# Strided attention and two expert layers on one core: half of a value load moved to ScalarE's queue, and the first weight chunk asked for one step earlier

## The chip, the cores and the metric

The kernel runs on one core of a Trainium2 chip. The metric is the time of one execution on the device in microseconds (us); the runs of the kernel before have their median at 618.33 us.

## The reference

All inputs are float32: q, k and v of 2 batches, 8 heads, 576 positions and 64 elements a head.

```python
scores = (q @ k.T) / sqrt(64)                 # per batch and head
mask   = (rel >= 0) & (rel < 32)              # heads 0-3, rel = i - j ("local")
mask   = (rel >= 0) & (j % 32 == i % 32)      # heads 4-7 ("strided")
attn   = softmax(where(mask, scores, -1e9)); x = attn @ v
x      = x laid out as 1152 tokens x 512
h      = ((x @ w1) * (x @ w2)) @ w3           # w1, w2: 512 x 1024, w3: 1024 x 1024
x      = h @ w_out                            # 1024 x 512
p      = domain_probs / (sum + 1e-9)          # 4 experts
out    = sum over e of p[:, e] * (relu(x @ W1[e]) @ W2[e])
```

## The kernel before

The program is one unrolled stream of instructions on each engine, in the order in which the Python code records them (a manual schedule): nothing reorders it, so what stands earlier in the source on one engine runs earlier there. The engines are TensorE (PE), VectorE (DVE), ScalarE (ACT) and GpSimd (POOL); SyncE (SP) issues nearly all loads and stores, as queue 1. ScalarE issues a few, as queue 10. Queue 8 and queue 14 carry instructions.

Attention of the first batch (`first`, six chunks; chunks 0 to 2 local heads, 3 to 5 strided heads) stands at the start and fills the first 24 us. Every chunk goes through `scores` (PE), `maxima` and `subtract` (DVE), `exps` or `slots_exps` (ACT), `sums` (DVE), `normalise` (POOL in this batch, L450), `transposes` (PE), `evac` (ACT, L460), `pv` (PE, L475 for local and L484 for strided heads) and `put` (ACT, L513). Then the product of x with w1 and w2 begins with `whole_product` (L616), which uses the first weight chunk `zero` in full float32; the other weight chunks are split into a high and a low float32r half on ACT and DVE, and the products of the second batch's attention are mixed in. After that come the combined matrix of w3 and w_out, and the experts, where PE is busy throughout.

The loads around the change, in SP's order: keys and queries of batch 0 (L322), the local values (`load_v_loc`, L330, 7 loads), the strided values (`load_v_str`, L352, two halves of 64 partitions, 320 KB each), their rest (`load_v_rest`, L357, two loads of 18 KB), then the first weight chunk (`zero.whole_load`, L160, two halves of 512 KB), the second chunk (L140), keys and queries of batch 1 (L322), and more chunks. Two things hold a load back. A load that must not start too early is tied to POOL: `hold` sets one column of its buffer (L128), and the load waits for that memset, which stands in POOL's stream behind whatever was recorded before it. And the loads take eight completion semaphores in turn (DMAHW0 to DMAHW7): the next load on a semaphore waits until the one before on it has landed.

The first weight chunk is used from `whole_steps` (DVE, L171 and on) and `whole_low` (ACT, L165).

Of the kernel before, what the change touches and what calls it, by code (L numbers as in the profile page):

```python
# [8 lines left out]
F32 = mybir.dt.float32  # L9
# [9 lines left out]
P = 128  # L19
# [25 lines left out]
def kernel(  # L45
# [13 lines left out]
    nc = tc.nc  # L59
# [10 lines left out]
    big = [tc.tile_pool(name=f"big{b}", bufs=4, side=side).__enter__() for b, side in enumerate(("right", "left"))]  # L70
# [241 lines left out]
    qk, vals = {}, {}  # L312
# [12 lines left out]
    def load_v_loc(b, c):  # L325

        tv = wp.tile([P, 2, 3, P], F32, tag="w", name="tv_loc")

        def load(dst, rows, t0, n):
            nc.sync.dma_start(out=dst, in_=v_loc[b, :, rows, t0:t0 + n].rearrange("k p t d -> p k t d"))  # L330

        lower, upper, middle = slice(0, 64), slice(64, P), slice(W, 3 * W)
        if c == 0:
            load(tv[lower, :, 0:1], lower, 0, 1)
            load(tv[upper, :, 0:1], middle, 0, 1)
            load(tv[:, :, 1:], slice(0, P), 1, 2)
        elif c == 1:
            load(tv, slice(0, P), 3, 3)
        else:
            load(tv[lower, :, 0:1], lower, 0, 1)  # L340
            load(tv[lower, :, 1:], middle, 1, 2)
            load(tv[upper], middle, 3, 3)
        vals[b, 0, c] = tv

    def load_v_str(b):

        tv = big[0].tile([P, 12, P], F32, tag="big", name="tv_str")
        row = 5 * P
        for k in range(2):
            at = v_str[b, k, 0, 0]  # L350
            rows = bass.AP(tensor=at.tensor, offset=at.offset, ap=[[row, 64], [T3 * row, 2], [1, row]])
            nc.sync.dma_start(out=tv[64 * k:64 * k + 64, :10].rearrange("p (h t) d -> p h (t d)", h=2), in_=rows)  # L352
        vals[b, 1] = tv

    def load_v_rest(b):
        for k in range(2):
            nc.sync.dma_start(out=vals[b, 1][64 * k:64 * k + NB, 10:], in_=v_str[b, k, 2 * T3:2 * T3 + NB, :2])  # L357
# [494 lines left out]
    with tc.manual_schedule():  # L852
# [5 lines left out]
        for i in range(4):  # L858
# [6 lines left out]
        load_v_loc(0, 0)  # L865
        load_v_loc(0, 1)
        load_v_loc(0, 2)
        load_v_str(0)
        load_v_rest(0)
        zero = c_w12[0]  # L870
        rest_loads = {5: [lambda: load_qk(1, 1)], 6: [lambda c=c: load_v_loc(1, c) for c in range(3)],
                      8: [lambda: load_v_str(1), lambda: load_v_rest(1)]}
        chunks = [[Chunk4(3 * g + c, b, g, c) for g in range(2) for c in range(3)] for b in range(B)]
        units = [(b, ft, i) for b in range(B) for ft in range(8) for i in range(2)]
# [52 lines left out]
        def exp_of(i):  # L927
            first[i].maxima()
            first[i].subtract()
            first[i].exps()  # L930

        def scale_of(i):
            first[i].sums()
            first[i].normalise()
# [14 lines left out]
        first[2].scores()  # L949
        first[1].maxima()  # L950
        first[1].slots_exps()
        scale_of(0)
        keep_warm(1, 2)
        first[3].scores()
# [7 lines left out]
        first[5].scores()  # L962
        first[0].pv()
        exp_of(3)
        scale_of(2)
        zero.whole_load()
        loaded = 1
        evac(1)
        first[2].transposes()
# [91 lines left out]
        for it in range(8):  # L1061
# [9 lines left out]
            if i is not None:  # L1071
# [7 lines left out]
        halves = [Tokens(0, 5, lambda name, i, n: ops.tile([P, 2, 320], F32R, tag="op", name=f"b_{name}{i}")),  # L1079
                  Tokens(5, 4, lambda name, i, n: keep(name, i, n))]  # L1080
        keeps = iter(range(9))

        def keep(name, i, n):

            k = next(keeps, None)
            if k is not None:
                return kept[:, k]
            return ops.tile([P, 2, 320], F32R, tag="op", name=f"b_{name}{i}")[:, :, :n]
# [121 lines left out]
```

## Time and profile before

| | us |
|---|---|
| median of 3 runs | 618.33 (617.79 to 619.99) |
| profiled execution, its own time | 618.26 |
| span of its trace | 616.1 |
| PE busy | 609.8 (99%) |
| DVE busy | 443.1 (72%) |
| ACT busy | 280.6 (46%) |
| POOL busy | 9.9 (2%) |

The span counts from the first to the last instruction of the core; 2.2 us of the time lie around it. Busy time is the union of an engine's instructions, weight loads of PE apart. The chain that ended last is followed backwards from the last instruction, at each step to what released it; a piece called issue is time in which the engine waited for nothing that the profile shows. The granted clock of PE is 1.00, its full level, in every stretch read here.

### The profile page before, as it was taken

The page shows a single profiled execution, that of the slowest core. Times are in us where ns is not written, and L with a number is a line of the kernel's source. Part 1 is how long each engine was busy: PE and PEld are TensorE (multiplying, and loading weights), DVE is VectorE, ACT ScalarE, POOL GpSimd, SP SyncE. Part 2 cuts the span into 40 slices and gives each one's busy share as a digit, 9 for nine tenths or more (in the row PEclk, how much of TensorE's full clock was granted, in tenths as well). Part 3 has the DMA queues.
Part 4 walks back from the last instruction along what each step waited for, and adds up shares of the span by engine and source line. Part 5 has one row for each costly group of instructions (what it writes and reads, how often), then busy time and mean ns, then how long its engine had stood idle before and what let it go on. Part 6 is the DMA issues. An engine that isn't in the chain of part 4 may idle for free.

```text
span 616.1 us, 11131 instructions
## 1 busy us (share of the span) xinstructions
PE 609.8 (99%) x4488; PEld 555.9 (90%) x4488; DVE 443.1 (72%) x811; ACT 280.6 (46%) x568; POOL 9.9 (2%) x33
## 2 busy tenths in 40 slices
PE   8999999999999999999999999999999999999997
PEld 5799999998889999998899988999889898989997
DVE  4899987998863237777877987887766665755843
ACT  3879966665733134333433333434343333333320
POOL 4100000000000000000000000000000000000000
PEclk9999999999999999999999999999999999999999
DMA  9896330334522202333545334435585557464411
GB/s 272 321 325 185 139 138 2 111 132 172 202 68 102 86 19 69 137 138 136 199 153 194 128 149 172 167 142 212 178 318 202 213 192 248 162 234 176 156 51 68
DMA packets 28510, 99.63 MB, mean 162 GB/s; under 512 B 2660, under 2 KB 6316, under 8 KB 26028
## 3 DMA queue, kind: packets, MB, share of 16 engines
q1 hardware_dynamic: 27916, 98.34, 44.5%
q8 instruction: 35, 0.57, 0.4%
q10 hardware_dynamic: 544, 0.59, 0.3%
q14 instruction: 15, 0.12, 0.1%
HBM read 79.78 MB, written 19.14 MB: 161 GB/s over the span
## 4 chain that ended last, share of the span: by engine, by line
PE 90%; DVE 4%; ACT 3%; DMA 2%; issue 1%; DVEq 0%; ACTq 0%; SPq 0%
PE g_acc L305 11%; PE g_acc L306 11%; PE g_acc L307 11%; PE m_a L307 4%; PE m_a L306 4%; PE m_a L305 4%; PE ab_acc L305 3%; PE ab_acc L307 3%; PE ab_acc L306 3%; PE m_b L306 3%; PE m_c L305 3%; PE m_c L306 3%; PE m_b L305 3%; PE x_acc L305 3%; PE m_c L307 3%; PE m_b L307 3%
## 5 line engine op out<-in xcount | busy, mean ns | idle before, releaser
L761 ACT ACTIVATE h_hi<-u 128x320 fp32r<-128x320 f32 (+1 forms) x128 | 56.9, 445 | 188.9 <-DVE u L767 188.9
L305 PE MATMUL g_acc<-w_hi,h_hi 128*128 128x512 f32 (+1 forms) x296 | 114.3, 386 | 0.0
L306 PE MATMUL g_acc<-w_lo,h_hi 128*128 128x512 f32 (+1 forms) x296 | 114.2, 386 | 0.0
L307 PE MATMUL g_acc<-w_hi,h_lo 128*128 128x512 f32 (+1 forms) x296 | 113.7, 384 | 0.0
L700 DVE TENSOR_TENSOR w_lo<-raw,w_hi 128x768 fp32r<-128x768 f32 x64 | 69.3, 1084 | 12.3 <-ACT w_hi L698 12.3
L767 DVE TENSOR_TENSOR u<-m_b,u 128x320 f32<-128x320 f32 (+1 forms) x96 | 40.7, 451 | 50.4 <-PE m_b L307 50.4
L305 PE MATMUL ab_acc<-x_hi,w_hi 128*128 128x288 f32 x240 | 71.6, 298 | 0.4 <-ACT ab L601 0.2
L307 PE MATMUL ab_acc<-x_hi,w_lo 128*128 128x288 f32 x240 | 70.7, 295 | 0.0
L306 PE MATMUL ab_acc<-x_lo,w_hi 128*128 128x288 f32 x240 | 70.7, 294 | 0.0
L307 PEld LDWEIGHTS g_acc<-w_hi,h_lo 128*128 128x128 f32 x296 | 55.6, 188 | 11.6
L305 PEld LDWEIGHTS g_acc<-w_hi,h_hi 128*128 128x128 f32 x296 | 55.8, 188 | 8.0
L306 PEld LDWEIGHTS g_acc<-w_lo,h_hi 128*128 128x128 f32 x296 | 55.7, 188 | 7.6
L763 DVE SCALAR_TENSOR_TENSOR h_lo<-u,h_hi 128x320 fp32r<-128x320 f32 (+1 forms) x128 | 57.6, 450 | 3.6 <-ACT h_hi L761 1.1
L698 ACT CAST w_hi<-raw 128x768 fp32r<-128x768 f32 x64 | 59.9, 936 | 0.0
L305 PEld LDWEIGHTS ab_acc<-x_hi,w_hi 128*128 128x128 f32 x240 | 45.0, 188 | 1.0 <-ACT ab L601 0.5
L306 PEld LDWEIGHTS ab_acc<-x_lo,w_hi 128*128 128x128 f32 x240 | 45.0, 188 | 0.0
L307 PEld LDWEIGHTS ab_acc<-x_hi,w_lo 128*128 128x128 f32 x240 | 45.0, 188 | 0.0
L306 PE MATMUL m_b<-b_t,s_hi 128*128 128x320 f32 (+1 forms) x128 | 37.9, 296 | 0.0
L767 DVE TENSOR_TENSOR u<-m_a,u 128x320 f32<-128x320 f32 (+1 forms) x64 | 28.8, 449 | 11.6 <-PE m_a L307 11.6
L700 DVE TENSOR_TENSOR s_lo<-raw,s_hi 128x1024 fp32r<-128x1024 f32 x16 | 19.6, 1225 | 24.3 <-ACT s_hi L698 24.3
L767 DVE TENSOR_TENSOR u<-m_c,u 128x320 f32<-128x320 f32 (+1 forms) x64 | 28.9, 452 | 4.5 <-PE m_c L307 3.9
L777 ACT COPY u<-m_a 128x320 f32<-128x320 f32 (+1 forms) x32 | 12.7, 398 | 42.4 <-PE m_a L307 42.4
(180 smaller groups left out, 1384.6 us busy)
## 6 DMA issues: line engine op xcount, KB each, us to landing
raw<-in_e_dram SPq DMA_DIRECT2D x32, 1024.0 KB, 4.9
raw<-in_w3T_dram SPq DMA_DIRECT2D x8, 1024.0 KB, 4.9
stored<-s_hi SPq DMA_DIRECT2D x16, 512.0 KB, 2.6
stored<-s_lo SPq DMA_DIRECT2D x16, 512.0 KB, 2.6
s_hi<-stored SPq DMA_DIRECT2D x16, 512.0 KB, 3.7
s_lo<-stored SPq DMA_DIRECT2D x16, 512.0 KB, 4.9
raw<-in_w_dram SPq DMA_DIRECT2D x7, 1024.0 KB, 7.2
raw<-in_w_out_dram SPq DMA_DIRECT2D x4, 1024.0 KB, 5.0
```

The lines of the kernel that those rows point to most:

```text
L305: mm(acc, lh, rh, start=first, stop=False)
L306: mm(acc, lh, rl, start=False, stop=False)
L307: mm(acc, ll, rh, start=False, stop=last)
L698: nc.scalar.copy(dst[0], src)
L700: nc.vector.tensor_tensor(out=dst[1], in0=src, in1=dst[0].bitcast(F32), op=ALU.subtract)
L761: nc.scalar.activation(hi, src, AF.Relu)
L763: nc.vector.scalar_tensor_tensor(out=lo, in0=src, scalar=0.0, in1=hi.bitcast(F32), op0=ALU.max, op1=ALU.subtract)
L767: nc.vector.tensor_tensor(out=out, in0=acc, in1=b, op=ALU.add)
L777: nc.scalar.copy(u1, a)
```

## The change

The upper half of the first batch's strided values (partitions 64 to 127) is no longer issued by SP ahead of the rest, but by ScalarE, behind the exponentials of chunk 1. The load of the first weight chunk, with its memset on POOL, is recorded ahead of the third normalising (`scale_of(2)`) instead of behind it.

```diff
-    def load_v_str(b):
-
-        tv = big[0].tile([P, 12, P], F32, tag="big", name="tv_str")
+    def load_v_str(b, halves=range(2), queue=nc.sync):
+
+        if (b, 1) not in vals:
+            vals[b, 1] = big[0].tile([P, 12, P], F32, tag="big", name="tv_str")
+        tv = vals[b, 1]
         row = 5 * P
-        for k in range(2):
+        for k in halves:
             at = v_str[b, k, 0, 0]
             rows = bass.AP(tensor=at.tensor, offset=at.offset, ap=[[row, 64], [T3 * row, 2], [1, row]])
-            nc.sync.dma_start(out=tv[64 * k:64 * k + 64, :10].rearrange("p (h t) d -> p h (t d)", h=2), in_=rows)
-        vals[b, 1] = tv
+            queue.dma_start(out=tv[64 * k:64 * k + 64, :10].rearrange("p (h t) d -> p h (t d)", h=2), in_=rows)
...
         load_v_loc(0, 2)
-        load_v_str(0)
+        load_v_str(0, (0,))
         load_v_rest(0)
...
         first[1].slots_exps()
+        load_v_str(0, (1,), nc.scalar)
         scale_of(0)
...
         exp_of(3)
+        zero.whole_load()
         scale_of(2)
-        zero.whole_load()
         loaded = 1
```

What this makes of the streams, with the semaphores that each instruction waits for (names as above; DVE_49, Pool_49 and the like stand for the other engines). On ScalarE, behind the six slot exponentials of chunk 1, before:

```order
L429 ACTIVATE p_ring,rec<-sc,mx 128x64 [waits PE_49,Activation_49,Pool_49]
L429 ACTIVATE p_ring,rec<-sc,mx 128x64 x5
L422 ACTIVATE p_ring<-p_ring 128x384 [waits DVE_49]
L460 COPY pT<-tp 128x384 [waits PE_49]
L422 ACTIVATE p_ring<-p_ring 128x8x54 [waits DVE_49]
```

and now:

```order
L430 ACTIVATE p_ring,rec<-sc,mx 128x64 [waits PE_49,Activation_49,Pool_49]
L430 ACTIVATE p_ring,rec<-sc,mx 128x64 x5
L354 DMA tv_str<-in_v_str_dram 64x2x640 [waits DMAHW0_49]
L423 ACTIVATE p_ring<-p_ring 128x384 [waits DVE_49]
L461 COPY pT<-tp 128x384 [waits PE_49]
L423 ACTIVATE p_ring<-p_ring 128x8x54 [waits DVE_49]
```

The load stands ahead of the exponential of chunk 2 and waits for DMAHW0, last used by the third local value load. On SP, from the last local value load to the second weight chunk, as a piece of the difference:

```order
-L352 DMA tv_str<-in_v_str_dram 64x2x640 [waits DMAHW5_49]
-L352 DMA tv_str<-in_v_str_dram 64x2x640 [waits DMAHW6_49]
-L357 DMA tv_str<-in_v_str_dram 18x256 [waits DMAHW7_49]
-L357 DMA tv_str<-in_v_str_dram 18x256 [waits DMAHW0_49]
-L160 DMA raw_405<-in_w_dram 128x1024 [waits DMAHW1_49,Pool_49]
-L160 DMA raw_405<-in_w_dram 128x1024 [waits DMAHW2_49]
+L354 DMA tv_str<-in_v_str_dram 64x2x640 [waits DMAHW5_49]
+L358 DMA tv_str<-in_v_str_dram 18x256 [waits DMAHW6_49]
+L358 DMA tv_str<-in_v_str_dram 18x256 [waits DMAHW7_49]
+L160 DMA raw_400<-in_w_dram 128x1024 [waits DMAHW1_49,Pool_49]
+L160 DMA raw_400<-in_w_dram 128x1024 [waits DMAHW2_49]
```

One strided half is gone, the two rest loads take the semaphores 6 and 7, and the weight chunk (`raw`) keeps 1 and 2, last used by the fourth and fifth local value load. On POOL, from the normalising of chunk 1, before:

```order
L413 MEMSET p_ring 128x8
L450 TENSOR_TENSOR p_ring<-p_ring,rec 128x384 [waits DVE_49,Activation_49]
L128 MEMSET raw_405 128x1
L413 MEMSET p_ring 128x8 [waits PE_49,Pool_49]
L450 TENSOR_TENSOR p_ring<-p_ring,rec 128x8x54 [waits DVE_49,Activation_49]
```

and now:

```order
L414 MEMSET p_ring 128x8
L128 MEMSET raw_400 128x1
L451 TENSOR_TENSOR p_ring<-p_ring,rec 128x384 [waits DVE_49,Activation_49]
L414 MEMSET p_ring 128x8 [waits PE_49,Pool_49]
L451 TENSOR_TENSOR p_ring<-p_ring,rec 128x8x54 [waits DVE_49,Activation_49]
```

The chunk's memset has changed places with the normalising of chunk 2. On PE only the semaphores for which the strided products wait have other numbers; DVE's stream is as it was.

## Rows read from the trace of the kernel before

**Rows 1.** The page: busy us (share of the span) and instructions of each engine.

```profile
PE 609.8 (99%) x4488; PEld 555.9 (90%) x4488; DVE 443.1 (72%) x811; ACT 280.6 (46%) x568; POOL 9.9 (2%) x33
```

**Rows 2.** The chain that ended last, first 35 us: start us, us, what.

```profile
13.28 0.90 issue
...
17.84 0.30 issue
```

**Rows 3.** DMA queues over the whole span: packets, MB, share of 16 engines.

```profile
q8 instruction: 35, 0.57, 0.4%
```

**Rows 4.** By stretch: us; busy PE, PEld, DVE, ACT, POOL; PEclk, DMA share, GB/s.

```profile
7.80:14.10 6.30, 5.48 (x131) 3.63 (x121) 4.88 (x14) 4.18 (x17) 1.74 (x4) 1.00 1.11 284
14.10:18.10 4.00, 3.66 (x127) 2.97 (x126) 3.40 (x7) 2.34 (x6) 1.85 (x5) 1.00 0.91 234
18.10:22.30 4.20, 4.16 (x121) 3.62 (x125) 3.83 (x8) 2.90 (x8) 2.03 (x4) 1.00 0.72 228
```

**Rows 5.** Queue 8 in 11.3:11.4, 15.3:15.4, 19.4:19.5 and 25.6:25.7 us.

```profile
q8 instruction: 1, 0.02, 85.5%
...
q8 instruction: 1, 0.02, 81.5%
...
q8 instruction: 1, 0.02, 57.9%
...
q8 instruction: 1, 0.02, 63.7%
```

**Rows 6.** The view by stretch again, cut by what the DMA engines do.

```profile
18.00:19.00 1.00, 0.86 (x15) 0.73 (x15) 0.96 (x3) 0.86 (x3) 0.39 (x1) 1.00 1.03 406
...
21.00:24.00 3.00, 2.71 (x74) 2.22 (x73) 2.50 (x5) 2.66 (x9) 0.00 (x0) 1.00 0.83 337
24.00:28.00 4.00, 4.00 (x18) 3.11 (x18) 3.13 (x6) 4.00 (x11) 0.00 (x0) 1.00 1.06 418
```

**Rows 7.** SP's issues in order of time: start us, us of all, what.

```profile
9.72 1.25 SPq L352 DMA_DIRECT2D tv_str<-in_v_str_dram  x2
11.01 0.90 SPq L357 DMA_DIRECT2D tv_str<-in_v_str_dram  x2
14.96 0.84 SPq L160 DMA_DIRECT2D raw<-in_w_dram  x2
19.58 0.33 SPq L140 DMA_DIRECT2D raw<-in_w_dram  x1
```

**Rows 8.** POOL in order of time: start us, us, what.

```profile
12.49 0.11 POOL L413 MEMSET p_ring<- 128x8 f32 x1
...
14.84 0.10 POOL L128 MEMSET raw<- 128x1 int32 x1
```

**Rows 9.** Loads issued near 5.4, 10.3 and 14.9: KB each, us to landing.

```profile
tv_loc<-in_v_loc_dram SPq DMA_DIRECT2D x1, 384.0 KB, 6.8
...
tv_str<-in_v_str_dram SPq DMA_DIRECT2D x2, 320.0 KB, 6.9
...
raw<-in_w_dram SPq DMA_DIRECT2D x1, 512.0 KB, 4.0
```

**Rows 10.** VectorE in order of time.

```profile
12.95 0.54 DVE L440 TENSOR_REDUCE rec<-p_ring 128x6 f32<-128x384 f32 x1
...
19.24 0.60 DVE L171 TENSOR_SCALAR w_whole<-raw 128x512 int32<-128x512 int32 x1
```

**Rows 11.** ScalarE in order of time.

```profile
10.56 0.23 ACT L429 ACTIVATION_READ_ACCUMULATOR p_ring<-sc,mx 128x1 f32 x1
11.31 0.53 ACT L422 ACTIVATE p_ring<-p_ring 128x384 f32<-128x384 f32 x1 [0.52 <-DVE p_ring L416]
...
22.86 2.26 ACT L513 COPY x_whole<-o 128x108 f32<-128x108 f32 x10
```

**Rows 12.** TensorE in order of time.

```profile
19.87 0.78 PE L484 MATMUL o<-pT,tv_str 54*64 54x54 f32 x32
...
23.03 0.81 PE L484 MATMUL o<-pT,tv_str 54*64 54x54 f32 x32 [0.29 <-ACT pT L460]
```

## The prediction

> **What bounds the kernel now.** I read first the page's busy times, then the chain of waits, then the queues. TensorE (PE) is busy 609.8 us, 99% of the span [rows 1], and from 23 us on the chain is its matmuls, or VectorE and ScalarE work that keeps step with them: whatever the first 23 us lose or gain reaches the end. So the question is which wait ends last in those 23 us. From the arrival of the first queries on, the chain there holds no load; it is PE's own work with two pieces called issue, 0.90 us at 13.28 and 0.30 us at 17.84 [rows 2], and at the end 0.29 us in which PE waits for a copy of ScalarE [rows 12]. In the two issue pieces PE stops between matmuls of the same line, which need nothing new.
>
> What they wait for is in the queues. Queue 8 moved 35 packets and 0.57 MB [rows 3], 16 KB each; PE ran 4488 matmuls and 4488 weight loads [rows 1], and 0.57 MB over 8976 instructions is 64 B each, so a packet is 256 PE instructions. Between the two stops PE ran 127 and 126 [rows 4], with a few semaphore instructions one packet. Counting one packet back from the first stop gives about 7.7 us, one forward from the second about 22.3 us [rows 4]. So PE stands still at the end of a block of instructions until the next one is in. In [rows 5] the packets of queue 8 begin in 11.3 to 11.4, 15.3 to 15.4, 19.4 to 19.5 and 25.6 to 25.7 us; share times 16 engines times 0.1 us gives their length: 1.37, 1.30, 0.93 and 1.02 us. Against the block boundaries 7.7, 14.2, 18.1 and 22.3 us the delay was 3.7, 1.2, 1.3 and 3.3 us. The long delays fell where the DMA engines were full (1.11 of their time in 7.8 to 14.1, 1.06 in 24 to 28), the short ones where queue 1 ran dry at times (0.91 in 14.1 to 18.1, 0.72 in 18.1 to 22.3, with the next load issued only at 19.58) [rows 4, 6, 7]. From a packet's begin to PE's restart it was 11.35 to 14.18 and 15.35 to 18.14, 2.8 us each; with the short packet of 19.4 I take 2.4.
>
> **The change part by part.** *First chunk asked for earlier.* The tiny memset that holds the load goes from 14.84 to behind the memset at 12.49 [rows 8], so about 12.6; its 0.10 us lies in the idle time of POOL, whose next work needs the sum that VectorE begins at 12.95 [rows 10]. The two issues of 14.96 (0.84 us for both) [rows 7] move to 12.7 and 13.1. They must wait for the loads that last used their semaphores, the fourth and fifth of the local values: the fourth, issued near 5.4, took 6.8 us to landing [rows 9], so 12.2; the fifth, a sixth of its size and issued 0.4 us later, should be there by 12.6. In time. SP has nothing else before 19.58. Does the earlier landing gain? The first half landed 4.0 us after 14.96, at 19.0; VectorE reads it at 19.24, and that row names no idle time before it [rows 9, 10]: VectorE was still at its sums. ScalarE's steps on it stand behind the copy of the fifth chunk and come later. Gain: 0.
>
> *Upper half on ScalarE's queue.* An issue of this form takes 1.25 us for two [rows 7], so 0.62 us. ScalarE is through with the slot exponentials at 10.79 and next wanted at 11.31 [rows 11]. Its issue waits for the 256 KB load of the first local values; the trace gives no landing, but SP's fourth strided issue, which waited for the same, went out by 11.6 (11.01 plus 0.90, less half) [rows 7]. So the issue ends between 11.4 and 12.2 and the exponential of the third chunk starts 0.1 to 0.9 us late. It ends by 12.8; VectorE's sum of it starts at 12.95 [rows 10], and the copy behind it feeds a value product that stands in PE's order behind the scores at which PE stopped, after 14.2. I take 0; without that cover it would be 0.9. The half was asked for at 10.36 and took some 7 us [rows 7, 9]; asked for at 11.3 it is there by 18.3 and wanted at 19.87 [rows 12]: 0. SP's two small loads go 0.6 us earlier: 0.
>
> *What the earlier chunk stands in front of.* The second block is asked for at 14.2. Before, queue 1 was then near its end, and the fetch began 1.2 us later. Now 1 MB has been asked for at 12.7, and it follows without a pause and occupies the engines until about 18.0 (15.4, when the strided values were through, plus 1.05 MB at the 0.406 MB/us of 18 to 19 [rows 6]). The price of a fetch into such traffic is bounded by 1.2 us (it passes by) and 3.7 us. I take 3.4, nearest to the fetch at 25.6, which stood behind big weight loads too. Restart: 14.2 + 3.4 + 2.4 = 20.0 instead of 18.1: **+1.9** (bounds 0 and, with 3.7 and 2.8, +2.6).
>
> The third block is then asked for at 20.0 instead of 18.1. Before, its fetch slipped into the pause between the two weight loads. Now it meets the next one, issued at 19.58 on the same cue as before, as POOL does not wait for this PE work; the engines are at 0.83 in 21 to 24 and 1.06 in 24 to 28 us [rows 6]. With 3.3 and 2.4 us PE gets it at 25.7; it reaches the boundary at 22.3 + 1.9 = 24.2. **+1.5** (bounds 0 and, with 3.7 and 2.8, +2.3). The fourth block, asked for at 25.7, has until 33 plus the shift: 0.
>
> *What comes back.* During the third stop ScalarE does work that was in PE's way: PE's 0.29 us wait at 23.03 goes [rows 12], and 4 of the 10 copies that take 2.26 us from 22.86 [rows 11] can be made early, 0.9 us. The work behind follows both, so I take 0.5 (bounds 0.3 and 0.9): **-0.5**.
>
> Sum: 1.9 + 1.5 - 0.5 = +2.9 us on the profiled execution's 618.26, so 621.2; the median of the three runs is 618.33, the same within 0.1. A measurement of this kernel can tell about 0.5%, 3.1 us, from no change.
>
> **Weighed against the trace.** In [rows 2] a block's end costs 0.90 and 0.30 us. The Trainium skill, "Runtime: NRT & Kernel Launch", section on instruction fetch mechanics, says that a sequencer fetches the next 16 KiB page by its own DMA queue and that crossing a boundary is mostly hidden; the block size agrees with [rows 3], the hiding does not hold in these 23 us. By that sentence the sum would be 0 and the time 618.3.
>
> **Rivals.** *Turns.* The fetch waits only for the share of the one load that its engine is moving. At 0.406 MB/us over 16 engines, 32 KB of a half chunk take 1.3 us; so it starts 0 to 1.3 us later than before, PE restarts at 18.7 to 19.4, and the third fetch, asked for by then, comes before the next chunk's data moves after 20.4. Total +0.6 to +1.3, 618.9 to 619.6. For it: nothing in the trace shows a fetch behind 4 KB rows. Against it: the first and fourth fetch let more than one load by. The Trainium skill, "DMA: Bandwidth & Descriptors", section on queues, rings and completion order, says an engine goes round the queues packet by packet; that is this rival, and the delays of 3.3 and 3.7 us speak against it.
>
> *Nothing or a little gained.* The fetch lands on an engine that is through, or the halves move better in two queues and everything is over sooner: from 0 to a gain of 0.6, the second stop and the wait for ScalarE: 617.7 to 618.4. For it: the second fetch of before did pass while the DMA engines were not yet idle. Against it: the first half chunk's share lies on all engines.
>
> *Slower by over 0.5%: strict order.* The fetch goes behind all that was queued before it. The second then starts when the chunk is through, 18.0 to 18.3, and PE restarts at 20.4 to 20.7 (+2.3 to +2.6); the third waits for the 1 MB of 19.58 and the keys and queries that SP asks for next (2.2 MB from 20.4 on at about 0.4 MB/us, so near 26), restart 28.4 against 24.8 wanted: +3.6. With 0.5 back +5.4, 623.7. It decides from a third fetch later than some 24.5 us. Against it: by 25.6, when the fourth fetch began, 3 us at 0.337 and 1.6 us at 0.418 MB/us make 1.7 MB [rows 6], less than the 2.2 MB asked for before it.
>
> *The change does not do what it says* would be the first chunk's issue held up on SP until 15 us; the semaphores above exclude it.
>
> **How the numbers follow.** Forecast, both stops: 0.45, from 619.9 (only the second stop) to 622.9 (3.7 and 2.8 us in both: +2.6 + 2.3 - 0.3). Turns: 0.25. Nothing or a little gained: 0.17. Strict order: 0.13. The range from 617.7 to 622.9 leaves out strict order, 0.13, and little else. Slower by over 3.1 us, above 621.4, are strict order and about 0.4 of the forecast's case: 0.13 + 0.18 = 0.31. Faster by as much needs a wait of 3.1 us that goes, and the two stops and ScalarE's wait together hold 1.5: 0.03 for what I don't see. The rest is 0.66.
>
> **What would show it.** Right: the chunk's issues near 12.7 us; queue 8's second packet starting at 17 to 18 instead of 15.35, its third at 23 to 24 instead of 19.45; issue pieces of about 2.2 us before PE's restart near 20 and of 1.5 us in the strided value matmuls; the first product matmul about 2.9 us after 23.8. VectorE's first step on the chunk stays at 19.2, ScalarE's exponential near 11.4. Wrong: a second packet before 16 us, or an end that does not follow the shift at 24 us. Were ScalarE held up beyond 13 us, the first part would be wrong as well.

## The result and the profile after

| | before | after |
|---|---|---|
| median, us | 618.43 (617.79 to 622.4, 7 runs) | 623.54 (623.08 to 626.06, 7 runs) |
| profiled execution, its own time / span, us | 618.26 / 616.1 | 623.14 / 621.2 |
| mean granted clock of PE in it | 1.00 | 0.994 |

The ratio is 1.0078, with a 95% interval of 1.0058 to 1.0098: the changed kernel is slower, by 5.1 us. The page (busy us, share of the span, instructions; then the granted clock in tenths, 40 slices) has 2.5 us more of busy PE than [rows 1], and one slice in which the clock is not full; the slice is 15.5 us long, so it is the one from 15.5 to 31 us:

```profile
PE 612.3 (99%) x4488; PEld 558.1 (90%) x4488; DVE 443.6 (71%) x811; ACT 280.5 (45%) x568; POOL 10.2 (2%) x33
...
PEclk9799999999999999999999999999999999999999
```

The small steps first. SP's stream of the changed kernel (start us, us of all, what), then the two halves of the chunk in the view of DMA issues (KB, us to landing, for 12.6 to 12.7 and 13.2 to 13.3 us):

```profile
12.60 0.84 SPq L160 DMA_DIRECT2D raw<-in_w_dram  x2
19.39 0.33 SPq L140 DMA_DIRECT2D raw<-in_w_dram  x1
```

```profile
raw<-in_w_dram SPq DMA_DIRECT2D x1, 512.0 KB, 6.5
...
raw<-in_w_dram SPq DMA_DIRECT2D x1, 512.0 KB, 7.3
```

The chunk is asked for 2.4 us earlier than in [rows 7], and its first half lands at 12.6 + 6.5 = 19.1 us; before it was 14.96 + 4.0 = 19.0 [rows 9]. Asking earlier brought nothing in earlier. ScalarE's and VectorE's streams (the last bracket is idle time and what ended it):

```profile
10.69 0.69 ACTq L354 DMA_DIRECT2D tv_str<-in_v_str_dram  x1
11.42 0.53 ACT L423 ACTIVATE p_ring<-p_ring 128x384 f32<-128x384 f32 x1 [0.69 <-DVE rec L446]
```

```profile
19.15 0.49 DVE L171 TENSOR_SCALAR w_whole<-raw 128x512 int32<-128x512 int32 x1
27.29 0.69 DVE L176 CUSTOM_DVE_ANT_0 w_whole<-raw,w_whole 128x1024 uint16<-128x1024 uint16 x1 [5.42 <-ACT raw L165]
```

The exponential of chunk 2 moves from 11.31 to 11.42, and VectorE starts on the chunk at 19.15 instead of 19.24 [rows 10, 11]. Its wait of 5.42 us is a consequence: ScalarE's step stands behind copies of PE's late results. The loss is in PE. The chain of waits (start us, us, what):

```profile
13.22 0.77 issue
13.98 0.30 PE sc L403 x3
...
16.94 0.70 PE o L476 x37
17.64 3.31 issue
20.96 0.63 PE o L476 x9
21.59 1.04 PE tp L456 x4
```

and queue 8 in 18.3 to 18.4 and 25.3 to 25.4 us:

```profile
q8 instruction: 1, 0.02, 64.1%
...
q8 instruction: 1, 0.02, 59.2%
```

The issue piece before the second block has grown from 0.30 [rows 2] to 3.31 us. I take it that the block is asked for at 13.98, where PE goes on into the block before it; no row shows the asking itself. Its packet begins near 18.37 instead of 15.39 (in the stretch 15.3 to 15.4 of [rows 5]), and takes 0.641 x 16 x 0.1 = 1.03 us. PE restarts at 20.96 instead of 18.14: **2.82 us**. The third packet begins near 25.36, and yet the chain has no third issue piece. What there is instead is in the view by stretch (us; busy PE, PEld, DVE, ACT, POOL; PEclk, DMA share, GB/s), first before, then after:

```profile
18.00:21.00 3.00, 2.86 (x99) 2.58 (x100) 2.85 (x7) 2.04 (x6) 2.03 (x4) 1.00 0.77 221
21.00:27.00 6.00, 5.71 (x86) 4.56 (x85) 4.67 (x9) 5.66 (x16) 0.00 (x0) 1.00 0.95 380
```

```profile
18.00:21.00 3.00, 0.04 (x4) 0.04 (x4) 2.83 (x7) 0.17 (x1) 2.31 (x4) 0.87 0.46 122
21.00:27.00 6.00, 6.00 (x103) 5.21 (x104) 0.84 (x2) 2.57 (x7) 0.00 (x0) 0.50 0.95 340
```

From 21 to 27 us the granted clock is 0.50, the lower level of 1.2 GHz; it was 1.00 before. TensorE's own rows of the same work, before and after (the last row of each is cut off at 30 us):

```profile
18.49 0.66 PE L455 MATMUL tp<-ident,p_ring 128*128 128x128 f32 x4
19.07 0.90 PE L475 MATMUL o<-pT,tv_loc 64*64 64x32 f32 x48
...
23.76 6.57 PE L616 MATMUL ab_acc<-x_whole,w_whole 128*128 128x288 f32 x26
```

```profile
21.52 1.11 PE L456 MATMUL tp<-ident,p_ring 128*128 128x128 f32 x4
22.56 1.51 PE L476 MATMUL o<-pT,tv_loc 64*64 64x32 f32 x48
...
28.93 1.24 PE L617 MATMUL ab_acc<-x_whole,w_whole 128*128 128x288 f32 x4
```

Four transposes take 1.11 instead of 0.66 us, 48 value products 1.51 instead of 0.90. From the restart to the first matmul of the whole product it was 23.76 - 18.14 = 5.62 us and is 28.93 - 20.96 = 7.97: **2.35 us**. The 5.62 held the wait of 0.29 us for ScalarE [rows 12]; now PE's rows have no wait in this stretch, so slower matmuls cost 2.64, and 0.29 of it came back. The two parts, 2.82 and 2.35, make 5.17 at the first whole product, against 621.2 - 616.1 = 5.1 in the span: all of the loss is there by 29 us, and none of it comes back later.

### The profile page after: what moved, and what is told of

It reads as the page before. It is cut to its first block, busy times and chain, and to the rows that moved or that the text cites. A ratio compares the mean times of both kernels' runs of the same rounds, so it can differ in the third digit from the quotient of the medians.

```text
span 621.2 us, 11131 instructions
## 1 busy us (share of the span) xinstructions
PE 612.3 (99%) x4488; PEld 558.1 (90%) x4488; DVE 443.6 (71%) x811; ACT 280.5 (45%) x568; POOL 10.2 (2%) x33
## 4 chain that ended last, share of the span: by engine, by line
PE 86%; DVE 5%; ACT 4%; DMA 2%; issue 2%; DVEq 0%; SPq 0%; ACTq 0%
PE g_acc L305 11%; PE g_acc L306 11%; PE g_acc L307 11%; PE m_a L307 4%; PE m_a L306 4%; PE m_a L305 4%; PE m_b L306 3%; PE m_c L305 3%; PE m_c L306 3%; PE m_b L305 3%; PE x_acc L305 3%; PE m_c L307 3%; PE m_b L307 3%; PE x_acc L306 3%; PE x_acc L307 3%; PE wc_acc L305 2%
## 5 line engine op out<-in xcount | busy, mean ns | idle before, releaser
L778 ACT COPY u<-m_a 128x320 f32<-128x320 f32 (+1 forms) x32 | 12.7, 398 | 42.2 <-PE m_a L307 42.2
```

The source lines that it names most:

```text
L778: nc.scalar.copy(u1, a)
```

## The experiments

My theory after the result (A): a fetch of instructions stands behind the bytes asked for before it, whatever the queue, so the earlier chunk makes the second stop; and a stop of some us is followed by a lower granted clock, which makes the rest. Rivals: the fetch only waits behind its own sort of queue, or the DMA engines' rate sets it; ScalarE's half has a part in it; the second half of the loss is the late third fetch, not the clock.

**The two parts alone.** e1 has only the chunk's move, e2 only the half on ScalarE's queue (a diff against the changed kernel, which puts the chunk back).

e1, against the kernel before:

```diff
         exp_of(3)
+        zero.whole_load()
         scale_of(2)
-        zero.whole_load()
```

e2, against the changed kernel:

```diff
         exp_of(3)
+        scale_of(2)
         zero.whole_load()
-        scale_of(2)
```

> The kernel before with the chunk's load alone ahead of the third normalising; both strided halves stay on SP. Theory A (PE's second block of instructions is fetched behind the chunk; PE stops, and its clock then falls): the whole loss is here. SP issues the chunk near 12.7 us, the second packet of queue 8 begins at 18 to 19 us instead of 15.35, PE stops some 3 us at 17.6, the granted clock falls to about 0.5 for some 7 us, time 623 to 624. Rival B (the load on ScalarE's queue does it, by a second queue that the fetch waits for): a packet at 15.3 to 16 us and 618 to 619.

> The changed kernel with the chunk's load put back behind the third normalising: only the upper half of the strided values goes by ScalarE. Theory A: second packet of queue 8 at 15.3 to 15.8 us, stop of 0.3 to 0.7 us, clock 1.00 throughout, time 618 to 619. Rival B: a stop of some 3 us and 623 to 624. A third case, both parts needed: here and with the chunk alone each 619 to 621.

Measured: e1 623.27 us, ratio 1.0073 (1.0059 to 1.0087); e2 618.43, ratio 0.9997 (0.9989 to 1.0006). The whole loss is the chunk's, and the half on ScalarE costs nothing. SP's and PE's rows of e1, and its view by stretch:

```profile
13.85 0.84 SPq L160 DMA_DIRECT2D raw<-in_w_dram  x2
...
19.57 0.42 PE L475 MATMUL o<-pT,tv_loc 64*64 64x32 f32 x11 [1.94 <-issue]
25.88 1.03 PE L484 MATMUL o<-pT,tv_str 54*64 54x54 f32 x45 [0.48 <-issue]
...
21.00:27.00 6.00, 5.52 (x135) 4.75 (x128) 3.12 (x7) 3.94 (x13) 0.00 (x0) 0.72 0.99 395
```

In e1 the strided half is still in SP's stream, and the chunk's issue waited for a landing until 13.85. PE asks for its block at 13.96, between the chunk's two halves: the fetch begins at 17.0, and the stop is 1.94, not the 3 us that I had expected. This profiled execution is e1's lightest, 621.17; its other executions took 622.12 to 624.19. Its clock is at half only from about 21.0 to 24.4 us, in the changed kernel from about 20.2 to 27.1. In e2 the clock is 1.00 throughout; queue 8 in 15.9 to 16.0 us and PE's stop:

```profile
q8 instruction: 1, 0.02, 76.2%
...
18.55 0.42 PE L476 MATMUL o<-pT,tv_loc 64*64 64x32 f32 x11 [0.57 <-issue]
```

**Half the dose.** e4 is the changed kernel with only the first 512 KB of the chunk asked for early.

```diff
...
+            if part:
+                hold(True, self.raw[:, 512, :1])
+                nc.sync.dma_start(out=flat(self.raw[:, 512:]), ...)
+                return
...
-            for i in range(2):
+            for i in range(1):
...
         scale_of(2)
+        zero.whole_load(1)
```

> The changed kernel with only the first half of the chunk (512 KB) ahead of the third normalising; the second half's memset and load stand behind it, as in the kernel before. Theory A, strictly in order of asking: the packet waits for half as much, begins near 16.9 us (between 15.4 of before and 18.4 of the changed kernel), PE restarts near 19.4, a stop of 1.8 us; whether the clock falls then is open: 619.8 without, up to 622.1 with. Rival D (turns between the queues, the fetch late only because both halves' shares were already taken up): packet before 16 us and 618.5.

Measured: 622.23 us, ratio 1.0057 (1.0044 to 1.007). Queue 8 in 16.9 to 17.0 us of e4, its PE, and its view by stretch:

```profile
q8 instruction: 1, 0.02, 63.6%
...
19.52 0.42 PE L480 MATMUL o<-pT,tv_loc 64*64 64x32 f32 x11 [1.94 <-issue]
...
21.00:27.00 6.00, 6.00 (x134) 5.28 (x138) 2.24 (x5) 3.12 (x9) 0.00 (x0) 0.53 0.96 377
```

**The other queue.** e8 is the changed kernel with the chunk's two loads issued by ScalarE, which is queue 10.

```diff
-                nc.sync.dma_start(out=flat(self.raw[:, c]), ...)
+                nc.scalar.dma_start(out=flat(self.raw[:, c]), ...)
```

> The changed kernel with both halves of the chunk issued by ScalarE, behind the exponential of the fourth chunk (near 13.6 and 14.1 us), so on the queue that SP's loads do not use. Theory A, in order of asking over all queues: the fetch asked for at 14.0, at its queue near 15.2, stands behind both halves; packet at 17 to 18.5 us, stop of 2 to 3.3 us, 622 to 624 with the clock's fall. Rival F (what delays it is queue 1's own backlog, and a second queue would be taken in turns with it): packet before 16.5 us and 618.5 to 619.5.

Measured: 623.51 us, ratio 1.0075 (1.0062 to 1.0088). ScalarE's issue and PE's stop:

```profile
13.22 1.07 ACTq L160 DMA_DIRECT2D raw<-in_w_dram  x2
...
20.90 0.42 PE L476 MATMUL o<-pT,tv_loc 64*64 64x32 f32 x11 [2.76 <-issue]
```

From the asking (the end of the first issue piece) to the packet's begin it is now, by how much of the chunk had been asked for by then:

| kernel | chunk's bytes asked for before | asked | packet begins | delay, us |
|---|---|---|---|---|
| before | 0 | 14.18 | 15.4 | 1.2 |
| e2 | 0 | 14.31 | 15.9 | 1.6 |
| e1 | 512 KB | 13.96 | 17.0 | 3.0 |
| e4 | 512 KB | 13.92 | 17.0 | 3.1 |
| e8 | 1 MB, queue 10 | 14.48 | 18.6 | 4.1 |
| after | 1 MB, queue 1 | 13.98 | 18.4 | 4.4 |
| e11 (below) | 1 MB, queue 1 | 13.89 | 18.5 | 4.6 |

Two amounts and two queues give one order for this fetch: it goes behind what was asked for before it. What is asked for just after it does not count: in e4 the second half goes out at 14.84, 0.9 us after the asking, and the delay is that of one half. Nor does the rate of the DMA engines alone tell these kernels apart: from 14 to 17 us they were at 1.08 of their time in e1, 1.07 in e4 and 1.06 in the changed kernel, and the delays are 3.0, 3.1 and 4.4. The rivals of the prediction by which it passes (turns between the queues, or nothing lost) fall with the rows of 512 KB and 1 MB.

Two packets of blocks that PE entered without a stop do not come out of this order as I count it. The fourth of the kernel before begins at 25.64, when 1.8 MB had moved since 19.58, although at least 2.2 MB had been asked for ahead of it; this is the objection that the prediction itself raised. And the third of e10 (below) begins at 20.42, though 1 MB had been asked for at 19.27 and PE comes to its block's start near 20.0. Whether these fetches passed by, or had been asked for earlier than I take it, no row shows.

**A stop without a moved load.** e3 and e10 are the kernel before, with one matmul of one column put in front of the second chunk's value products. It reads the weight chunk as loaded, its second half in e3 and its first half in e10, and so waits for that landing; the value products overwrite what it writes. No load moves.

```diff
+            if self.index == 1 and not self.b:
+                mm(banks[0][:, :1], ident, zero.raw[:, 1023, 1:].bitcast(F32), start=True, stop=True)
```

(In e10 the index is 511.)

> The kernel before, no load moved, with one matmul of one column ahead of the second chunk's value product, into a bank that this product then overwrites; it reads the second half of the first weight chunk, so PE waits from 16.9 us until that half has landed, near 20.3 us. It tells the stop from its reason. Theory A with the clock: PE stops 3.3 us, in place of the 0.3 us stop of before, and the granted clock falls to about 0.5 for some 7 us as in the changed kernel, which costs 2.3 us more: 618.3 + 3.0 + 2.3 = 623.6. Rival C (the stop alone is the price, the 2.3 us behind it come from something else, such as loads in the way): clock 1.00 and 621.3.

> The kernel before with the matmul of one column that reads the first half of the chunk instead of the second, so that PE waits from 16.9 until near 19.1 us: a stop of about 2 us with no load moved, as long as those behind half a chunk. Theory A with the clock: the granted clock falls as in those, for 3.4 or 6.8 us, 621 to 622.5. Rival C: it holds, and 620.2.

Measured: e3 624.5 us, ratio 1.0096 (1.0081 to 1.011); e10 623.98, ratio 1.0085 (1.0071 to 1.0098). PE's rows and the view by stretch, of e3 and of e10:

```profile
20.87 0.56 PE L469 MATMUL o<-raw,ident 128*128 128x1 f32 x2 [3.98 <-DMA raw<-in_w_dram]
...
21.00:27.00 6.00, 6.00 (x138) 5.49 (x139) 1.10 (x2) 1.67 (x5) 0.00 (x0) 0.50 0.99 397
```

```profile
18.99 0.35 PE L469 MATMUL o<-raw,ident 128*128 128x1 f32 x2 [2.16 <-DMA raw<-in_w_dram]
20.45 1.11 PE L455 MATMUL tp<-ident,p_ring 128*128 128x128 f32 x4
21.50 1.51 PE L477 MATMUL o<-pT,tv_loc 64*64 64x32 f32 x48
...
21.00:27.00 6.00, 6.00 (x122) 4.98 (x123) 1.54 (x4) 2.65 (x7) 0.00 (x0) 0.55 0.94 345
```

A stop of another kind brings the same clock, and rows of the same length (1.11 and 1.51) as in the changed kernel. e10's stop takes 2.16 us and its first whole product comes at 28.08, 4.32 later than before; so the slow stretch costs about as much as the stop again. Rival C falls with both. The sizes were missed: e3's stop is 3.98 us instead of 3.3, and both times lie above what I had put down.

**Clock or third fetch.** In the changed kernel the third packet is late too: asked for at 20.96, begun at 25.36. At full clock PE would have been at that block's end near 25.4 (the same stretch takes 18.50 to 22.95 in e12, below), and the packet would have let it go on near 27.8: a stop of 2.4, hardly more than the 2.35 that the clock took. The two lie beside each other. e11 takes the late fetch away: the second chunk and what follows it on SP are held back until queue 1 has run dry.

```diff
-            nc.gpsimd.memset(ap, 0)
+            (nc.vector if held == 2 else nc.gpsimd).memset(ap, 0)
...
         scale_of(4)
-        load_next(True)
...
-        load_qk(1, 0, held=True)
-        load_next()
...
-        zero.whole_steps(0)
+        zero.whole_steps(0, lambda: load_next(2))
+        load_qk(1, 0, held=True)
+        load_next()
```

(The load in `whole_steps` stands ahead of the last step on the chunk's first half.)

> The changed kernel, in which the second weight chunk and the loads behind it are asked for only about 21.9 us into the span (held by a memset on VectorE behind four of the chunk's steps) instead of at 19.4. In the changed kernel two things fall together: TensorE's granted clock is 0.50 from 20.3 to 27.1 us, and the third fetch of instructions begins only at 25.4, so that its block would have been late at full clock too. Here queue 1 is empty when the third block is asked for near 21.0. Theory (the clock alone is enough for the loss behind the second stop): the stop before 21.0 is 3.3 us as it was, the third fetch begins by about 22.2 us, the clock is 0.50 all the same, and the first product matmul stays at 28.7 to 29.0; 623 to 624 us. Rival (the late third fetch sets the pace): the first product matmul comes at 26.4 to 26.7 and the time at 620.9 to 621.5.

Measured: 623.48 us, ratio 1.0068 (1.005 to 1.0087). Queue 8 in 22.2 to 22.3 us of e11, then PE, then the view by stretch:

```profile
q8 instruction: 1, 0.02, 85.2%
...
20.87 0.42 PE L477 MATMUL o<-pT,tv_loc 64*64 64x32 f32 x11 [3.31 <-issue]
24.14 1.11 PE L457 MATMUL tp<-ident,p_ring 128*128 128x128 f32 x4
28.78 4.39 PE L618 MATMUL ab_acc<-x_whole,w_whole 128*128 128x288 f32 x17
...
21.00:27.00 6.00, 6.00 (x109) 5.06 (x111) 1.29 (x4) 2.82 (x7) 0.00 (x0) 0.56 0.70 205
```

The third fetch now begins at 22.2, long before it is needed, and the first whole product still comes at 28.78 (28.93 in the changed kernel). The clock alone is enough for the second part of the loss: 28.78 - 20.87 = 7.91 us from the restart, against 7.97 in the changed kernel and 5.62 before.

**A late third fetch at full clock.** e12 is the kernel before with the second chunk asked for one normalising earlier, so that only the third fetch has more in front of it.

```diff
         scale_of(3)
+        load_next(True)
...
         scale_of(4)
-        load_next(True)
```

> The kernel before, with the second weight chunk asked for one normalising earlier on GpSimd, at about 17.7 us instead of 19.6, so that 1 MB more stands in front of the third fetch of instructions and nothing more in front of the second. Theory (a fetch stands behind all that was asked for before it, and a stop of 2 us and more is followed by a lower clock): the second fetch stays at 15.4 and the stop of 0.3 us with it; the third, asked for at 18.1, begins at 22 to 23 us instead of 19.4; TensorE stops for 2.2 to 3.0 us in the strided value matmuls before 25.4, and its granted clock falls for some us behind that; 621.5 to 624 us. Rival (the stop costs its own length and the clock stays 1.00): 620.6 to 621.4. Rival (the fetch passes by the load): no stop, 618.3 to 618.8.

Measured: 621.78 us (619.13 to 624.45), ratio 1.0047 (1.0027 to 1.0067). Queue 8 in 21.9 to 22.0 us of e12, then PE:

```profile
q8 instruction: 1, 0.02, 55.8%
...
24.27 1.03 PE L484 MATMUL o<-pT,tv_str 54*64 54x54 f32 x45 [1.32 <-issue]
25.23 8.03 PE L616 MATMUL ab_acc<-x_whole,w_whole 128*128 128x288 f32 x32
```

The fetch begins 3.4 us after it is asked for (18.50) instead of 1.3: the order holds for this block too. The stop is shorter than either theory gave, 1.32, and in the profiled execution, of 619.7 us, the clock stays full. The median lies higher because most other executions have a lower mean clock; their clocks and times fall in three groups:

| mean clock of the execution | times, us |
|---|---|
| 0.999 to 1.0 | 619.13, 619.7, 619.85 |
| 0.997 | 620.88, 621.66, 621.89 |
| 0.995 | 623.12, 623.28, 623.46, 624.45 |

So the clock falls in some executions and not in others, and those with a lower mean clock take 2 to 4 us longer (means of the groups 619.6, 621.5 and 623.6). Only the one of 619.7 us was traced: where in the others the clock fell, and how long their stops were, is not shown.

**Looking for a version that beats both.** If fetches stand behind loads, later loads should free them. e7 is the kernel before with the second and third local values and the strided values asked for behind `exp_of(0)`, held by a memset on VectorE. e6 does this as well, and lets ScalarE issue the upper strided half behind `exp_of(3)`. e9 adds to e6 that the chunk is asked for in halves, the first held by VectorE, the second behind `scale_of(3)`. The edit of e7:

```diff
-        load_v_loc(0, 1)
-        load_v_loc(0, 2)
-        load_v_str(0)
-        load_v_rest(0)
...
         exp_of(0)
+        load_v_loc(0, 1, True)
+        load_v_loc(0, 2)
+        load_v_str(0)
+        load_v_rest(0)
```

> A version that uses theory A: the chunk's load where it was before; the loads of the second and third local values, and SP's strided loads, are held by a one-column memset on VectorE until the first chunk's subtraction, near 7.9 us, and ScalarE asks for the upper strided half only behind the exponential of the fourth chunk, near 13.6 us. Theory A: the first fetch, asked for near 7.6, has less in front of it and begins near 9.5 instead of 11.3 us, so the stop at 13.2 us (0.9) goes; the second, asked for near 13.2, has 320 KB less in front and begins near 15, a stop of 0 to 0.6 us; clock 1.00; 617.2 to 618.2, hardly to be told from the kernel before by time, but by the stops. Rival E (the strided lower half and the fetch meet later, so the second stop grows by what the first loses): 618.3 to 619.5.

> The kernel before with the later local values alone (both strided halves on SP behind them). Theory A: first packet near 9.5 us and no stop at 13.2, as in the version with both parts; but the second fetch, asked for near 13.2, stands behind both strided halves, which end near 15.6: it begins near 15.6 us, PE restarts near 18.3 against 17.0 wanted, a stop of 1.3 us, in sum the time of before, 618.3, if the clock holds, and some 620 to 621 if such a stop lets it fall. Rival E': the first stop goes, the second stays at 0.3: 617.4.

> The version with the later values (both early stops gone, but a third stop of 1.21 us at 21.2, where the third block's fetch, asked for at 16.4, stood behind the whole chunk asked for at 14.8, and VectorE 2.16 us idle for the chunk) with the chunk's two halves apart: the first held by VectorE's memset behind its third sum, near 13.6 us, the second by POOL's behind the fourth normalising, near 16.8 us, so after the third fetch is asked for. Theory A: third packet of queue 8 near 17.7 to 18.5 instead of 19.96 us, no stop over 0.3 us up to the first product, that product's first matmul near 22.5 instead of 23.57 us (23.76 in the kernel before), clock 1.00, 617.0 to 617.6 and few executions above 619. Rival G: the second block's fetch, asked for near 12.9, now meets the first half: a stop of 1 us at 16.4 and 618.5 to 621; or the halves come too late for VectorE and 618.3.

Measured: e6 618.66 us, ratio 1.0011 (0.9995 to 1.0028); e7 620.16, ratio 1.0019 (1.0004 to 1.0034); e9 618.89, ratio 1.0003 (0.9994 to 1.0012). The PE rows with their waits, of e6 (and its view by stretch, in which the granted clock is 0.50), of e7 and of e9:

```profile
22.38 1.03 PE L487 MATMUL o<-pT,tv_str 54*64 54x54 f32 x45 [1.21 <-issue]
23.57 8.74 PE L619 MATMUL ab_acc<-x_whole,w_whole 128*128 128x288 f32 x28 [0.16 <-DVE w_whole L176]
...
24.00:27.00 3.00, 3.00 (x7) 2.09 (x7) 2.76 (x6) 2.86 (x5) 0.00 (x0) 0.50 1.07 422
```

```profile
17.89 0.42 PE L477 MATMUL o<-pT,tv_loc 64*64 64x32 f32 x11 [1.12 <-issue]
22.85 1.03 PE L486 MATMUL o<-pT,tv_str 54*64 54x54 f32 x45 [0.50 <-issue]
```

```profile
17.24 0.42 PE L482 MATMUL o<-pT,tv_loc 64*64 64x32 f32 x11 [0.43 <-issue]
22.19 1.03 PE L491 MATMUL o<-pT,tv_str 54*64 54x54 f32 x45 [0.50 <-issue]
```

In each of them the first stop is gone (0.90 us before), and a later one comes in its place: e6 stops 1.21 us ahead of the third block, which its theory did not have, e7 1.12 ahead of the second (1.3 expected). In e6's profiled execution the clock falls behind a stop of 1.21 us; in e12's it stayed full behind 1.32. e9 reaches the first whole product at 23.15, 0.6 earlier than before, and its median is not lower, so its 617.0 to 617.6 was missed. In e6 and e7, some executions have a mean clock of 0.994 to 0.997 and take 619.3 to 622.1 us (617.1 to 618.8 with a full clock). None of these beats the kernel before beyond what can be measured, and e7 is slower by 0.04 to 0.34%; a version that is faster than both was not found.

## Why the prediction failed

*Bound and place: right.* What the first 23 us lose reaches the end: +5.17 at the first whole product, +5.1 in the span.

*The steps off PE: right.* The chunk is issued at 12.60 (12.7 predicted), ScalarE's exponential starts at 11.42, VectorE's first step at 19.15. Zero for the half on ScalarE's queue (e2: 0.9997), and zero gain from the earlier chunk: it landed at 19.1 against 19.0. The DMA engines had been at 1.11 of their time from 7.8 to 14.1 before [rows 4], and in the changed kernel they are at 1.06 from 14 to 17; so the chunk's bytes had to wait there instead of in SP's stream.

*"A fetch into such traffic ... I take 3.4", +1.9: right mechanism, mis-sized.* The delay was 4.4 and the restart 20.96, +2.8, above the upper bound of +2.6. The failing choice was to go by the nearest row of before, 3.7 us at most, although the rival of strict order had the better rule: the packet begins when the chunk is through, which it put at 18.0 to 18.3 (18.37 measured). Runs with 0, 512 KB and 1 MB in front give delays of 1.2 to 1.6, 3.0 to 3.1 and 4.1 to 4.6 us.

*"+1.5" for a third stop: did not happen; of "-0.5" only the wait of 0.29 us came back.* The third fetch was late as the text had it, by more (25.36, against 23 to 24; a delay of 4.4 against the 3.3 in the sum). But PE arrived there late as well, since its clock was at half: no issue piece. The wait for ScalarE went as predicted, but the ten copies still start only 0.9 us ahead of the whole product (28.04 and 28.93, before 22.86 and 23.76), so none of them was made early. In place of +1.5 - 0.5 = +1.0 stand 2.64 of slower matmuls less 0.29, +2.35.

*What no term held: the clock.* The rows on which the prediction rests have a full clock before, next to the stops of 0.30 and 0.90 us, and its sum carries this over, without a reason, to a PE that was to stand still for 2.2 us and stood for 3.3. e3 and e10 show with no load moved that such a stop is followed by half clock, and e11 that this alone makes the loss behind the stop. The Trainium skill, "TensorE: Matmul & The Clock Gate", section "HAM oscillation — how this bites in real kernels", tells of waits for DMA in a stream of matmuls that bring TensorE back to the lower clock; the rows here agree in direction (0.50 after the stop of 3.31 us, 0.55 after e10's 2.16). It would have been a reason to put a lower clock behind the new stop among the rivals, and none of them had it.

*The rivals.* Turns and the two without loss fall with the table of delays. The Trainium skill, "DMA: Bandwidth & Descriptors", section on queues, rings and completion order, by which an engine goes round the queues packet by packet, does not describe the second fetch here: with 1 MB ahead of it on queue 10 the packet of queue 8 begins 4.1 us after the asking, with 1 MB on queue 1 after 4.4. Strict order named 623.7 us, next to the 623.54 measured, but with a wrong second half: it has a third stop of 3.6 us, which no row shows, so its nearness is in part luck. Its second block is right; the objection to it, the fourth fetch of before, still stands for that fetch. *The chances* failed with this: all of the cases left the clock at 1.00, so the range ended at 622.9.

What stays open: why the clock falls in some executions of one kernel and not in others (e12, e6, e7, and at times the kernel before: one of its executions beside e1 took 621.43 us at a mean clock of 0.992); when a fetch is asked for if PE does not stop; and what a late third fetch would cost the changed kernel if its clock stayed full. That was only worked out (2.4 us), and by it the loss would be about as large without the clock.

## What to carry to other kernels

Where a long unrolled stream starts with small matmuls, look at the queue that carries instructions: a load asked for earlier than it is needed can hold up the next block of instructions, though the load itself comes in no sooner. Before putting a stop of TensorE into a sum at its own length, ask what clock follows it: in the traced executions stops of 1.9 to 4.0 us cost 1.2 (e1) to 2.4 us (e4, e8) more behind them, counted from the restart to the whole product against the 5.62 us of before. Ask for a load when the engines have room for it, not when its buffer is free.

## What the runs showed of the hardware that was not expected

- A 16 KB fetch of instructions on queue 8 can stand behind loads asked for before it on queue 1 or on queue 10: it began 1.2 to 1.6, 3.0 to 3.1 and 4.1 to 4.6 us after the asking with 0, 512 KB and 1 MB in front of it. Not every packet fits (the fourth of before and e10's third do not).
- Where PE stopped for a block, it went on 1.2 to 1.6 us after the packet's end (18.37 + 1.03 = 19.4 to 20.96 in the changed kernel, 21.9 + 0.9 = 22.8 to 24.27 in e12, 18.58 + 1.07 = 19.65 to 20.90 in e8).
- The granted clock fell to 0.50 in or behind stops of 1.21 (e6), 1.94 (e1, e4), 2.16 (e10), 2.76 (e8), 3.31 (after, e11) and 3.98 us (e3); it stayed at 1.00 behind 1.32 (e12) and 1.12 (e7) in the traced executions. At half clock four 128x128 transposes took 1.11 instead of 0.66 us and 48 value products 1.51 instead of 0.90, 1.7 times as long and not twice.
